# One output unit of a fused attention and feed-forward kernel: three plain output tiles, or two tiles by seven half-size products and a third spread around them

## Chip, cores and metric

The kernel runs on one core of one Trainium2 chip. The metric is the device time of one execution in microseconds. Five runs of the kernel before gave a median of 212.53 us (212.46 to 215.06).

## What is computed

A sparse attention over 4 batches, 8 heads, 768 positions and a head dimension of 64, followed by a feed-forward layer on the 3072 rows of 512 that it gives.

```python
# attention: a window of 16 positions to each side, and 24 block summaries (max of k, mean of v)
k_sum = k.reshape(B, H, nb, 32, D).max(axis=3)
v_sum = v.reshape(B, H, nb, 32, D).mean(axis=3)
scores_l = where(|i - j| < 16, scale * q @ k.T, -1e9)
scores_s = scale * q @ k_sum.T + log(32)
a = softmax(concatenate([scores_l, scores_s]))
x = a @ concatenate([v, v_sum])            # heads side by side: 3072 x 512
# feed-forward
h = x @ w_in                               # 512 -> 2048
out = (h * sigmoid(1.702 * h)) @ w_out     # 2048 -> 512, float32
```

## The kernel before

The 3072 rows are worked in eight units of 384 rows (`HALF`), two to a batch: unit u belongs to batch u // 2, and its half is u % 2. Each unit has three row tiles of 128. `ff_in(u, nts)` multiplies the transposed activations `xT[u % 2]` with `w_in` (64 matmuls of width 384 into the PSUM tiles `ph`) and ScalarE applies the gelu into `gT[u % 2]`.

The second matrix product is done in two ways. `ff_out(u, ms, part)` does a quarter of a plain output tile: four matmuls of width 512 into a PSUM bank `po`; after the fourth quarter ScalarE copies the bank to `osb` and SyncE stores it. `Pair(ta, tb, ss)` forms two row tiles together as a two by two block product by seven half-size products instead of eight (`p1` to `p7`): every product is eight matmuls of width 256, and VectorE forms the sums of the gT quarters (`sums`, into `ss`, and in place in gT), the sums of the `w_out` quarters (`w_sums`, into `ta` and `tb`) and the additions of PSUM results into `osb`. Banks `px`, `pw` and `py` hold running sums. Before the change, units 0 and 1 use `ff_out` throughout, and units 2 to 7 use pairs.

The attention of the next unit or batch is spread between the output steps. After output step `slot` of unit u, `beside(u + 1, slot)` issues what `plan1` (or `plan0`) lists there: `t` transposes q on TensorE, `s` and `S` are `scores` of a pair of heads (12 matmuls listed as `ps_s`, an exponential on ScalarE into `a_sb`, a multiplication with a mask on VectorE), `v` is `values` of two pairs (24 matmuls `ps_av`, then on VectorE a reciprocal and a multiplication for each pair, into `x2`), and `x` transposes the result on TensorE into `xT`. The last results of the stage go to `xT` by transposing transfers, `dx`, issued on SyncE's queue; so do keys (`xk`) and queries (`xq`) of batch 2. POOL's queue loads k, q and v and copies the halo rows of the values inside SBUF (`vw<-vw`, `vw<-vs`).

Order on each engine is the program's order (`_Ordered`). PSUM has eight banks: the pool `pmm`, tag "mm", has four one-bank tiles (`ph`, `po`, `px`, `pw`, `py`, and the small transposes), and the pool `psb`, tag "big", has two two-bank tiles (scores, the q transposes, and value matmuls when `values` is called with `big`). `beside` called `values` with `big` in unit 0's stage (u == 1 there) and without it in unit 1's, the one that is changed:

```python
elif what[0] == "v":
    values(b, half, i, u == 1)
```

Of the kernel before, what the change touches and what calls it, by code (L numbers as in the profile page):

```python
# [11 lines left out]
F16 = mybir.dt.float16  # L12
# [23 lines left out]
def kernel(  # L36
# [25 lines left out]
    JH = NJ // 2  # L62

    pe = _Ordered(tc, nc.tensor)
    dve = _Ordered(tc, nc.vector)
    act = _Ordered(tc, nc.scalar)
# [5 lines left out]
    stage = ctx.enter_context(tc.tile_pool(name="stage", bufs=1))  # L72
# [8 lines left out]
    raw, early = {}, {}  # L81
# [266 lines left out]
    def halo_dmas(w5, j0):  # L348
        halo_odd(w5, j0)
        halo_even(w5, j0)  # L350
# [88 lines left out]
    def q_turn(p, half=0):  # L439
        src = cast.pop(("q", p))  # L440
        ps = pmm.tile([128, 512], F32, name="ps_q", tag="mm")
        st["Q", p] = ps
        for r in range(JH):
            pe.matmul(out=ps[:, r * 128:r * 128 + 128] if half else at(ps, r, [[JH, 128]]),
                      lhsT=src[:, r].rearrange("p h d -> p (h d)"),
                      rhs=ident, start=True, stop=True)
# [136 lines left out]
    def xk(g, b):  # L583
        s = b % 2
        k4 = kxs[s].rearrange("p i (j e) c -> p (i j) e c", e=2)
        src = rows["k", b][:, 2 * g:2 * g + 2].rearrange("p i j h d -> p (i j h d)")
        for e in range(2):
            sp.dma_start(out=k4[:, 2 * g * NJ:2 * (g + 1) * NJ, e, e * 64:e * 64 + 64],
                         in_=src[e * 64:e * 64 + 64], transpose=True)
# [15 lines left out]
    def tq1(p, eng):  # L605
        copy(eng, qT[p][1], trans(rows["q", 1][:, p].rearrange("p j h d -> p j (h d)")))
# [13 lines left out]
    def values(b, half, g, big=False):  # L620

        pvs = []
        for i in range(2):
            p = 2 * g + i
            a = a_sb[p]
            if big and i == 0:
                ps = psb.tile([128, 1024], F32, name="ps_av", tag="big")
            one = (ps[:, i * 512:i * 512 + 512] if big else
                   pmm.tile([128, 512], F32, name="ps_av", tag="mm"))
            pv = one[:, 0:390].rearrange("p (h j c) -> p h j c", h=2, j=JH)  # L630
            pvs.append(pv)
            for hh in range(2):
                for j in range(JH):
                    for e in range(2):
                        t = 2 * j + e
                        pe.matmul(out=pv[e * 64:e * 64 + 64, hh, j, :], lhsT=a[:, hh, t, :],
                                  rhs=vw[b % 2][:, half * TH + t, 2 * p + hh, 0:D + 1],
                                  start=True, stop=True, skip_group_check=True)
        x2[g] = attp.tile([128, 2, JH, 2, D], F16, name="x2", tag="x2")
        for i in range(2):  # L640
            norm(x2[g][:, i], pvs[i])

    def norm(x, pv):
        rc = attp.tile([128, 2, JH, 1], F32, name="rc", tag="rc")
        dve.reciprocal(out=rc, in_=pv[..., D:D + 1])
        dve.tensor_mul(x.rearrange("p j h d -> p h j d"), pv[..., 0:D],
                       rc.to_broadcast([128, 2, JH, D]))
# [42 lines left out]
    def ff_out(u, ms, part):  # L690
        if part == 0:
            po_now[ms] = pmm.tile([128, d_model], F32, name="po", tag="mm")
        po = po_now[ms]
        for nt in range(4 * part, 4 * part + 4):
            pe.matmul(out=po, lhsT=gT[u % 2][:, nt, ms * 128:(ms + 1) * 128],
                      rhs=w_out_sb[:, nt, :], start=(nt == 0), stop=(nt == NT - 1))
        if part == 3:
            osb = outp.tile([128, d_model], F32, name="osb", tag="osb")
            act.activation(out=osb, in_=po, func=ACT.Copy)
            r0 = u * HALF + ms * 128  # L700
            sp.dma_start(out=out[r0:r0 + 128, :], in_=osb)

    NI, DH = NT // 2, d_model // 2
    ts = {}

    def w_sums(c):

        if c == 0:
            w = w_out_sb.rearrange("p (i e) d -> p e i d", e=2)
            b11, b12, b21, b22 = (w[:, e, :, x * DH:(x + 1) * DH] for e in range(2) for x in range(2))  # L710
            ta = stage.tile([128, 2, NI, DH], F16, name="ta", tag="tA")
            tb = stage.tile([128, 2, NI, DH], F16, name="tb", tag="tB")
            ts.update(b11=b11, b12=b12, b21=b21, b22=b22, t1=ta[:, 0], t2=ta[:, 1], t3=tb[:, 0],
                      t4=tb[:, 1])
        for x, y, z in (("t1", "b12", "b11"), ("t2", "b22", "t1"), ("t3", "b22", "b12"),
                        ("t4", "b21", "t2")):
            dve.tensor_sub(*(ts[n][:, 2 * c:2 * c + 2] for n in (x, y, z)))
# [6 lines left out]
    def product(ps, a, b, first):  # L724
        for i in range(NI):
            pe.matmul(out=ps[:, 0:DH], lhsT=a[:, i], rhs=b[:, i], start=(first and i == 0),
                      stop=(i == NI - 1), skip_group_check=True)

    def bank(name):
        return pmm.tile([128, d_model], F32, name=name, tag="mm")  # L730
# [6 lines left out]
    class Pair:  # L737
# [51 lines left out]
            self.w = bank("pw")  # L789
            product(self.w, self.a21, ts["t3"], True)  # L790

        def p2(self):
            y = bank("py")
            product(y, self.a12, ts["b21"], True)
            dve.tensor_add(self.osb(0)[:, 0:DH], y[:, 0:DH], self.t1)
            self.store(0, 0, False)

        def p4(self):
# [8 lines left out]
    def gelu_soon():  # L807

        act.activation(out=gate[:, 1:2], in_=gate[:, 0:1], func=ACT.Gelu_apprx_sigmoid)
# [122 lines left out]
    for p in range(NP):  # L932
# [5 lines left out]


    plan1 = {0: ["t0"], 1: ["t1"], 2: ["s0", "s1"], 4: ["t2"], 5: ["t3"],  # L940
             6: ["v0", "s2", "s3"], 8: ["x0"], 9: ["v1", "S0", "S1"], 11: ["x1", "S2", "S3"]}

    plan0 = {-1: ["q0", "q1", "q2", "q3", "s0", "s1"], 3: ["v0", "s2"], 5: ["x0", "s3"], 7: ["v1"], 9: ["x1"]}

# [2 lines left out]
    def beside(u, slot):  # L947
        b, half = u // 2, u % 2
        for what in (plan0 if u == 1 else plan1).get(slot, ()):
            i = int(what[1])  # L950
            if what[0] == "t":
                tq1(i, dve if i % 2 else act)
            elif what[0] == "q":
                q_turn(i, 1)
                q_copy(i, dve, 1)
            elif what[0] == "s":
                scores(b, half, i)
                if half and i == NP - 1:
                    gelu_soon()
            elif what[0] == "S":  # L960
                scores(b, 1, i)
                if i == NP - 1:
                    gelu_soon()
            elif what[0] == "v":
                values(b, half, i, u == 1)
            else:
                tx(i, half)

    for u in range(2):
        todo = {}  # L970
        if u == 0:
            for p in range(NP):
                todo.setdefault(12 + p // 2, []).append(lambda p=p: cast_q(dve, p, 1))
        else:
            def value_rows():
                vsum(1, range(NJ))
                block_sums()
                halo_dmas(w51, 0)
                sum_dmas(w51, 0)
                load_vc(2)  # L980
                load_qc(2)

            todo = {0: [lambda: tk(0, 1)], 3: [lambda: tk(1, 1)], 5: [lambda: v_odd(1)],
                    6: [lambda: tk(2, 1)], 9: [value_rows], 11: [lambda: tk(3, 1)]}
            ff_in(u, range(3))
        for nt in range(0 if u else N0, NT):
            if u == 0 or nt > 2:
                ff_in(u, (nt,))
            for f in todo.get(nt, ()):
                f()  # L990
        exp_soon()
        if u == 0:
            beside(1, -1)
            load_qc(1)
            load_kc(2)
            busy(6)
        order = [(ms, part) for ms in range(JH) for part in range(4)]
        if u == 0:

            order = [(ms, part) for part in range(4) for ms in range(JH)]  # L1000
        for i, (ms, part) in enumerate(order):
            ff_out(u, ms, part)
            beside(u + 1, i)
            if u == 0 and i in (4, 7, 10):
                w_sums(i // 3 - 1)
            if u == 1 and i == 2:
                w_sums(3)
            if u == 1 and i == 3:
                for g in range(2):
                    xk(g, 2)  # L1010

    order = ["a7", "a2", "a6", "b1", "a5", "b7", "a3", "a4", "b6", "b2", "b5",
             "c1", "b3", "c7", "c6", "c2", "c5", "b4", "c3", "c4"]
# [16 lines left out]
    for b in range(1, B):  # L1030
        n, s = b + 1, (b + 1) % 2
        more = n < B
        ss = stage.tile([128, NP - 1, 2, NI, 128], F16, name="ss", tag="vf")
        u = 2 * b
# [85 lines left out]
```

## Time and profile before

| | |
|---|---|
| Median of five runs | 212.53 us |
| Profiled execution, its own time | 212.8 us |
| Its span, first to last instruction | 210.8 us |
| TensorE clock granted | 1.000 throughout |
| TensorE matmuls busy | 201.6 us, 96% of the span |
| VectorE, ScalarE, POOL busy | 134.3, 122.2, 94.7 us |
| Unit 1's output stage on TensorE | 61.3 to 76.8 us of the span |
| TensorE idle before unit 3 | 1.10 us, waiting for xT |

Times in the text are microseconds from the start of the span unless they are durations. A row of the chain has start, length, engine, tile and number of instructions. A row of a timeline has start, length, engine, operation, tiles out<-in and shape; in brackets stands the idle time before it and what ended it. A matmul row's length includes the drain of the array; the distance between starts is what one costs in a stream.

### The profile page before, as it was taken

To read this page: it belongs to the slowest core of one execution; us is meant where nothing else is said; L and a number is where in the kernel's file an instruction comes from. 1 tells how busy PE (TensorE), PEld (TensorE's weight loads), DVE (VectorE), ACT (ScalarE), POOL (GpSimd) and SP (SyncE) were. 2 spreads that over 40 slices of the span, in tenths; PEclk is the share of its full clock that TensorE was granted. 3 is DMA by queue.
4 is the path that set the end of the run, shared out by engine and by line. 5 is a ranking of instruction groups with operands and counts; after the bars stand their busy time and mean duration, and the time that the engine had idled before them with its cause. 6 is when DMAs were issued, how large, how long until landed. Compare 5 with 4: busy or idle time off the path is not lost.

```text
span 210.8 us, 5499 instructions
## 1 busy us (share of the span) xinstructions
PE 201.6 (96%) x2193; PEld 136.8 (65%) x2193; DVE 134.3 (64%) x394; ACT 122.2 (58%) x228; POOL 94.7 (45%) x173
## 2 busy tenths in 40 slices
PE   7879999999999999899999999999999999999993
PEld 2656565556555556455888875566888865668882
DVE  7489956587976679934767780599757710366332
ACT  2674778155676388657824567677444667772220
POOL 8878989799999931503999201220000000000000
PEclk9999999999999999999999999999999999999999
DMA  5999999999999999999999999992043250000223
GB/s 149 308 164 195 234 252 222 177 149 215 175 160 137 159 151 173 160 162 118 111 126 192 168 180 192 192 132 47 3 137 90 68 159 0 3 0 25 82 77 118
DMA packets 96610, 29.33 MB, mean 139 GB/s; under 512 B 84481, under 2 KB 93601, under 8 KB 96585
## 3 DMA queue, kind: packets, MB, share of 16 engines
q0 software_dynamic: 67920, 14.88, 79.8%
q1 hardware_dynamic: 28664, 14.11, 34.4%
q8 instruction: 17, 0.28, 0.6%
q14 instruction: 9, 0.07, 0.1%
HBM read 27.26 MB, written 6.29 MB: 159 GB/s over the span
## 4 chain that ended last, share of the span: by engine, by line
PE 68%; POOL 13%; DMA 12%; SPq 2%; DVE 2%; issue 2%; POOLq 0%
PE ph L28 28%; PE px L28 15%; PE pw L28 8%; PE po L28 5%; DMA xT<-x 4%; PE py L28 4%; DMA kb<-in_k_dram 3%; PE ps_s L28 3%; PE ps_av L28 3%; POOL qb L28 3%; DMA qf<-in_q_dram 2%; POOL mk L28 2%; POOL kb L28 2%; DMA kq<-in_k_dram 2%; SPq L28 2%
## 5 line engine op out<-in xcount | busy, mean ns | idle before, releaser
L28 PE MATMUL ph<-xT,w_in_sb 128*128 128x384 f16 x512 | 86.3, 326 | 1.2 <-DMA xT<-x 1.1
L28 ACT ACTIVATE gT<-ph 128x384 f16<-128x384 f32 x128 | 61.0, 491 | 27.2 <-PE ph L28 27.0
L28 PEld LDWEIGHTS <-w_in_sb 128*128 128x128 f16 x512 | 49.3, 98 | 33.8 <-DMA xT<-x 1.5
L28 PEld LDWEIGHTS <-gT 128*128 128x128 f16 x384 | 35.6, 98 | 12.4
L28 ACT ACTIVATE a_sb<-ps_s 128x768 bf16<-128x768 f32 x28 | 21.2, 806 | 11.4 <-PE ps_s L28 11.4
L28 PE MATMUL po<-w_out_sb,gT 128*128 128x512 f16 x96 | 23.1, 380 | 0.0
L28 PEld LDWEIGHTS <-ss 128*128 128x128 f16 x216 | 20.9, 98 | 2.6
L28 DVE TENSOR_TENSOR a_sb<-a_sb,mk 128x768 bf16<-128x768 bf16 x28 | 15.6, 557 | 10.0 <-ACT a_sb L28 8.4
L28 DVE TENSOR_TENSOR ss<-gT 128x512 f16<-128x512 f16 (+3 forms) x21 | 8.0, 381 | 21.0 <-ACT gT L28 20.9
L28 ACT ACTIVATE t<-px 128x256 f32<-128x256 f32 x21 | 8.1, 385 | 20.2 <-PE px L28 20.2
L28 PE MATMUL pw<-tb,gT 128*128 128x256 f16 x144 | 18.7, 273 | 0.0
L28 PE MATMUL px<-ta,ss 128*128 128x256 f16 x144 | 18.7, 273 | 0.0
L28 DVE TENSOR_REDUCE ks<-kx 128x24 bf16<-128x768 bf16 x12 | 11.3, 945 | 8.1 <-DMA kx<-kb 8.1
L28 POOL DMA_DIRECT2D vw<-vw x12 | 6.5, 558 | 22.2 <-DVE vw L28 14.3
L28 DVE TENSOR_TENSOR x<-ps_av,rc 128x384 f16<-128x384 f32 x28 | 15.6, 558 | 1.0
L28 POOL DMA_DIRECT2D vw<-in_v_dram x18 | 15.9, 933 | 0.0
L28 POOL DMA_DIRECT2D kb<-in_k_dram x16 | 13.2, 851 | 1.9 <-DMA w_out_sb<-in_moe_w_out_dram 1.4
L28 POOL DMA_DIRECT2D qb<-in_q_dram x16 | 13.3, 928 | 1.1 <-DMA vw<-in_v_dram 1.1
L28 DVE TENSOR_TENSOR osb<-pw,t 128x256 f32<-128x256 f32 x18 | 7.6, 423 | 9.2 <-PE pw L28 5.1
L28 ACT ACT_TABLE_LOAD x10 | 12.8, 1283 | 1.0 <-PEq L1104 0.8
L28 PE MATMUL ps_s<-qT,kx 64*128 64x64 bf16 (+3 forms) x400 | 9.5, 190 | 1.0 <-DVE qT L28 1.0
L28 PEld LDWEIGHTS <-kx 64*128 64x128 bf16 x400 | 7.4, 94 | 4.6 <-issue 3.9
(103 smaller groups left out, 247.0 us busy)
## 6 DMA issues: line engine op xcount, KB each, us to landing
out_dram<-osb SPq DMA_DIRECT2D x18, 256.0 KB, 5.0
vw<-in_v_dram POOLq DMA_DIRECT2D x18, 128.0 KB, 5.4
w_in_sb<-in_moe_w_in_dram POOLq DMA_DIRECT2D x4, 512.0 KB, 8.9
w_out_sb<-in_moe_w_out_dram POOLq DMA_DIRECT2D x4, 512.0 KB, 16.8
kf<-in_k_dram SPq DMA_DIRECT2D x8, 192.0 KB, 4.3
kb<-in_k_dram POOLq DMA_DIRECT2D x16, 96.0 KB, 4.7
qb<-in_q_dram POOLq DMA_DIRECT2D x16, 96.0 KB, 7.1
out_dram<-osb SPq DMA_DIRECT2D x12, 128.0 KB, 1.7
```

Source lines behind the costliest of these rows:

```text
L28: r = f(*a, **kw)
```

## The change

In unit 1, row tiles 0 and 1 are formed by a `Pair`, and tile 2 by `ff_out`, with its four quarters as steps 2, 3, 4 and 11 of the twelve. `sums` of the pair and its first addition (`c11`, split off from `p2`) follow step 1. The last part of the weight sums, `w_sums(3)`, moves ahead of the stage. One step holds no output work. In `plan1`, `x0` moves from step 8 to 7, and `v1`, `S0`, `S1` from 9 to 8. `values` always takes a "big" PSUM tile. The key transposes `xk` of batch 2 stay after step 3, but no output tile is finished by then. The sums take the staging buffer "vf" before batch 1's pairs use it.

```diff
-        def p2(self):
-            y = bank("py")
-            product(y, self.a12, ts["b21"], True)
-            dve.tensor_add(self.osb(0)[:, 0:DH], y[:, 0:DH], self.t1)
+        def p2(self, early=False):
+            self.y = bank("py")
+            product(self.y, self.a12, ts["b21"], True)
+            if not early:
+                self.c11()
+
+        def c11(self):
+            dve.tensor_add(self.osb(0)[:, 0:DH], self.y[:, 0:DH], self.t1)
             self.store(0, 0, False)
...
     plan1 = {0: ["t0"], 1: ["t1"], 2: ["s0", "s1"], 4: ["t2"], 5: ["t3"],
-             6: ["v0", "s2", "s3"], 8: ["x0"], 9: ["v1", "S0", "S1"], 11: ["x1", "S2", "S3"]}
+             6: ["v0", "s2", "s3"], 7: ["x0"], 8: ["v1", "S0", "S1"], 11: ["x1", "S2", "S3"]}
...
             elif what[0] == "v":
-                values(b, half, i, u == 1)
+                values(b, half, i, True)
...
-        order = [(ms, part) for ms in range(JH) for part in range(4)]
         if u == 0:
-
-            order = [(ms, part) for part in range(4) for ms in range(JH)]
-        for i, (ms, part) in enumerate(order):
-            ff_out(u, ms, part)
-            beside(u + 1, i)
-            if u == 0 and i in (4, 7, 10):
-                w_sums(i // 3 - 1)
-            if u == 1 and i == 2:
-                w_sums(3)
-            if u == 1 and i == 3:
-                for g in range(2):
-                    xk(g, 2)
+            for i in range(12):
+                ff_out(0, i % JH, i // JH)
+                beside(1, i)
+                if i in (4, 7, 10):
+                    w_sums(i // 3 - 1)
+
+    ss = stage.tile([128, 2, NI, 128], F16, name="ss", tag="vf")
+    pair = Pair((1, 0), (1, 1), ss)
+    w_sums(3)
+    for i, step in enumerate(("p2", "p1", 0, 1, 2, "p7", "p6", "p5", None, "p3", "p4", 3)):
+        if step == "p2":
+            pair.p2(True)
+        elif step == "p1":
+            pair.p1(act)
+        elif step in (0, 1, 2, 3):
+            ff_out(1, 2, step)
+        elif step:
+            getattr(pair, step)()
+        beside(2, i)
+        if i == 1:
+            pair.sums(0, NI)
+            pair.c11()
+        if i == 3:
+            for g in range(2):
+                xk(g, 2)
```

## Prediction

> **What bounds the kernel now.** I read the busy shares first, then the chain that ended last, then the waits of the stage that is edited, then ScalarE, SyncE and the transfers beside it. All instructions go through one helper (L28), so groups are told apart by tile.
>
> ```profile
> span 210.8 us, 5499 instructions
> PE 201.6 (96%) x2193; PEld 136.8 (65%) x2193; DVE 134.3 (64%) x394; ACT 122.2 (58%) x228; POOL 94.7 (45%) x173
> ```
>
> TensorE is the bound: whatever shortens or stalls its list moves the end. The chain, in order of time (start, length, what), shows the edited stage (output of unit 1, 61.3 to 76.8) and what follows:
>
> ```profile
> 62.48 0.86 PE po L28 x4
> ...
> 69.23 0.50 PE ps_av L28 x24
> 69.73 0.46 PE ps_s L28 x24
> 70.19 1.83 PE po L28 x8
> 72.02 0.34 PE ps_x L28 x6
> ...
> 79.74 2.60 PE ph L28 x16
> 82.33 8.81 DMA xT<-x
> 91.19 9.59 PE ph L28 x58
> 100.77 0.87 PE px L28 x8
> ```
>
> Inside the stage TensorE goes from one piece to the next without a gap. The chain leaves it only at 82.33: unit 3 waits for its transposed activations xT. TensorE's timeline shows the price, and the list of transfers their time to landing:
>
> ```profile
> 89.95 2.37 PE L28 MATMUL ph<-xT,w_in_sb 128*128 128x384 f16 x12 [1.10 <-DMA xT<-x]
> ```
>
> ```profile
> xT<-x SPq DMA_TRANSPOSE x2, 8.9
> ```
>
> 1.10 us before 89.95, and, since the second tile landed 0.25 us after the first six matmuls, 1.35 us in all. So a shift of TensorE before 88.85 isn't simply a shift of the end: 1.35 us here belong to the transfers. Beside TensorE in the stage, ScalarE and SyncE's queue:
>
> ```profile
> 64.87 1.51 ACT L28 ACTIVATE a_sb<-ps_s 128x768 bf16<-128x768 f32 x2 [0.84 <-PE ps_s L28]
> ...
> 70.06 1.51 ACT L28 ACTIVATE a_sb<-ps_s 128x768 bf16<-128x768 f32 x2 [2.04 <-PE ps_s L28]
> ```
>
> ```profile
> 66.90 0.33 SPq L28 DMA_DIRECT2D out_dram<-osb  x1
> 67.47 8.67 SPq L28 DMA_TRANSPOSE kx<-kq  x4
> 76.23 2.16 SPq L28 DMA_DIRECT2D out_dram<-osb  x2
> 80.95 2.86 SPq L28 DMA_TRANSPOSE xT<-x  x2
> ```
>
> Two score groups are exponentiated one behind the other (0.81 us each, 0.70 apart) while TensorE has 1.8 us of output matmuls to do. SyncE's queue is in order: the four key transposes stand behind the first output store, which waited for ScalarE's copy of the first tile.
>
> **The change, part by part.**
>
> *TensorE's products.* Removed: 12 chunks of four 512-wide matmuls at 0.86 to 0.87 (chain rows), 10.4. Added: seven products of eight 256-wide matmuls at 0.87 (row px x8), 6.1, and four chunks, 3.45. Gain 0.85 us; bounds 0.8 and 0.9. Each 256-wide matmul needs its own weight load, 98 ns by the page's group of ss loads, under the 109 ns that a matmul lasts, so nothing is added. The Trainium skill, TensorE: Matmul & The Clock Gate, section Back-to-back issue gap, speaks against the change: it gives sustained spacings of 81 ns at width 128 and 131 ns at 512, hence, as an estimate between, some 97 ns at 256; by it 56 x 97 + 16 x 131 stand against 48 x 131 and the change would lose 1.2 us. This trace has 216 ns at 512 and 109 at 256, and decides.
>
> *First product.* py needs odd gT columns up to the last gelu, which ends at 61.81; its eighth matmul would come at 61.9. Up to 0.15 us; I take 0.1.
>
> *VectorE and ScalarE.* Added on VectorE: three sums of 128x1024 and one more in p6 (0.67 to 0.69 each on the three rows at 89.59), three adds of 0.42 from PSUM, 4.0 us; w_sums(3) only moves forward, to 61.8. VectorE is busy 11.4 of 17.7 us here, so 15.4 fit. The last sum (a21, which p7 reads) ends near 66.3 and p7 starts near 67.1: covered by 0.8 us, and each 0.1 beyond costs 0.1. ScalarE gets four copies of 0.385 for two of 0.60: +0.3, in idle time.
>
> *Score buffers: the new wait.* The value matmuls now take a "big" PSUM tile, of which there are two, instead of two "mm" banks (those hold px, pw, po and the transposes). In plan1, v0, s2, s3 follow each other without TensorE work between, and so do v1, S0, S1. The value tile is held until VectorE has normalised it (1.5 us, rows at 69.58 to 71.06), so both score groups share the other buffer: in the built program's order the first matmul of the second group waits for ScalarE, the exponential of the first. From 64.48, the first score matmul, to 64.87 is 0.39, the exponential 0.81, a semaphore 0.04: the second group can start 1.24 after the first where it now starts at 0.23. That is 1.0 us, twice: 2.0. Behind it on TensorE's in-order list stands the rest of the stage. Bounds: 0 if the buffers were given out otherwise, 2 x 1.5 if a group waited for the normalisation instead; the order names ScalarE, so 2.0.
>
> *Late masks.* s3 is late, so its exponential and mask (0.81 + 0.56) end 1.8 after its matmuls begin; p5, x0 and the first half of v1 cover 0.23 + 0.87 + 0.34 + 0.25 = 1.7. Wait 0.1 to 0.4; I take 0.3. S0, S1 have p3, p4 and a chunk behind them: nothing; without these it would be 1.8 too.
>
> *SyncE's queue and the halos.* POOL's list is unchanged, its key, halo and value transfers from 53 to 70 included; SyncE keeps the same number, but no output store stands ahead of the key transposes. They wait only for k of batch 2, whose first four heads land by 61.5. So they issue from 61.8 rather than 67.5 and meet the value halos that v0 needs (vw<-vw, vw<-vs, the last landing 67.55 against v0 at 69.2: cover 1.6). The trace doesn't show this meeting. Nearest rows: two halo copies issued at 126.15 near transposes landed in 5.4 us against 4.9 (+0.5: no wait); those at 86.3 to 89.3, behind a backlog, took 8.2 to 10.6 against 4 to 5 (+3.4 to +6.4: a wait of 1.8 to 4.8). It is nearer the first in backlog, the second in number of transposes: +2.4, wait 0.8. Cover gone, each us late is a us. The Trainium skill, DMA: Bandwidth & Descriptors, section Queues, rings and completion order, says that an engine alternates between queues packet by packet, a half share. By that, an estimate: 4.2 us of halo traffic left would take 8.4 and v0 wait 2.6.
>
> *The xT wait.* Unit 2 now starts 0.85 less and 0.1 + 2.0 + 0.3 + 0.8 more, 2.35 us later; its transposes issue at 83.3 and 84.7, and TensorE reaches unit 3 at 91.2. No wait if the first lands within 7.9 us and the second within 7.5. Bounds: 2.8 us (the transpose at 155.28, little beside it) and 8.9 as now. Now the key transposes hold the queue until about 82 and two stores until 86; begun 5.7 us earlier, they end near 75 and three stores follow by about 82. I take under 7.5: the 1.35 goes. If not, it stays. Stores, q loads and xT share the same engines, but what is moved is the same in sum.
>
> Sum: -0.85 + 0.1 + 2.0 + 0.3 + 0.8 - 1.35 = +1.0 us. The profiled execution took 212.8, 2.0 around its span; it is 0.27 above the median of 212.53, so I add the sum to the median: 213.5.
>
> **Rivals.** (a) xT still takes 8.9 us, as the queue is only reshuffled: no slack comes back, +2.35, 214.9. For it: DMA engines are busy in nine tenths or more of nearly all of 61 to 92; against: the queue ahead is shorter. (b) Halos come 3 us after v0's turn, as behind the backlog at 86: +3.2, 215.7, and up to 217.5 at 4.8. (c) No halo wait, the rest as forecast: +0.2, 212.7; for it the row at 126.15. (d) Faster: the two score groups get separate buffers, so the one exchange of banks costs nothing. Then the stage is 0.85 - 0.1 shorter and the xT wait also falls: -0.75 - 1.35 = -2.1, 210.4. It decides as soon as the second score matmul starts within 0.3 us of the first; the program's order speaks against it. (e) That the products don't save their columns: the widths are in the list; no share.
>
> **How the numbers follow.** Forecast 0.42, with a range of its own from 212.8 to 214.7; (a) 0.26; (b) 0.15; (c) 0.11; (d) 0.06. A measurement of this kernel can tell about 1% from no change, 2.1 us: 210.4 to 214.65. Faster: half of (d), 0.03. Slower: (a), (b) and 0.04 of the forecast's upper edge, 0.45. Same: 0.52. The range leaves out (d), the upper third of (b) and a little of (c): 212.5 to 216.3.
>
> **What would show it.** In the profile after: two TensorE gaps near 1.0 us ahead of score matmuls, released by ScalarE's a_sb; a gap of 0.3 ahead of value matmuls, and one ahead of v0 released by a vw transfer; key transposes from about 61.8; unit 2's first ph near 79.1 instead of 76.73; no gap at unit 3. Wrong if the score groups stand side by side, if the xT gap is still over 1 us, or if v0 doesn't wait.

## The result, and the profile after

Against the kernel before, the changed kernel took 1.0084 of the time (95% interval 1.0062 to 1.0106), which on the median of 212.53 us is 214.3 us; measured again beside two variants it was 1.0071 (1.0038 to 1.0105). That is 0.8% more: the interval lies above 1, but the step is under the 1% within which the forecast called a kernel the same. (The comparison uses only executions within 1.5% of the fastest of each kernel; the plain medians over all of them, 216.69 us after and 213.19 before, lie 1.6% apart, because it leaves out 23 of 40 executions after and 7 of 77 before.)

The profiled execution took 214.23 us. Its page, the span and the busy shares:

```profile
span 212.5 us, 5559 instructions
PE 201.7 (95%) x2217; PEld 140.0 (66%) x2217; DVE 136.5 (64%) x401; ACT 122.7 (58%) x230; POOL 94.2 (44%) x173
```

TensorE is busy 201.7 us where it was 201.6, although work was saved, and the span is 1.7 longer. The first reason is not in the edited stage. A table by stretches (stretch, its length, busy time of PE, PEld, DVE, ACT and POOL, the granted clock, the DMA share, GB/s) has half clock long before it, in code that both kernels share:

```profile
12.00:16.40 4.40, 3.25 (x72) 2.31 (x71) 3.89 (x8) 3.35 (x4) 3.58 (x10) 1.00 2.15 170
16.40:19.90 3.50, 3.23 (x60) 1.99 (x60) 1.96 (x4) 0.81 (x1) 3.43 (x6) 0.51 1.23 200
```

Unit 1's output stage therefore starts at 62.31 instead of 61.12, 1.19 us late. So I count places in the stage from its first matmul, here the first `py`, before the first `po`. TensorE's timeline of the stage:

```profile
62.31 1.04 PE L28 MATMUL py<-w_out_sb,gT 128*128 128x256 f16 x8
...
70.39 0.57 PE L28 MATMUL ps_av<-vw,a_sb 128*64 128x65 bf16 x24
70.89 0.35 PE L28 MATMUL ps_s<-qT,kx 64*128 64x64 bf16 x12
72.14 0.35 PE L28 MATMUL ps_s<-qT,kx 64*128 64x64 bf16 x12 [0.90 <-ACT a_sb L28]
...
75.55 0.35 PE L28 MATMUL ps_s<-qT,kx 64*128 64x64 bf16 x12 [0.90 <-ACT a_sb L28]
...
79.34 2.12 PE L28 MATMUL ph<-xT,w_in_sb 128*128 128x384 f16 x12
```

The 24 score matmuls that stood together before are now two groups of 12 with 0.90 us of idle time between them, twice, both ended by ScalarE's exponential. Unit 2's first `ph` comes 17.03 us after the stage's first matmul; before it came after 15.61. The stage has grown by 1.42. The chain that ended last now goes through those two waits, and then stays on TensorE where it used to leave for xT:

```profile
71.28 0.82 ACT a_sb L28
72.10 0.04 issue
72.14 0.35 PE ps_s L28 x12
...
74.69 0.82 ACT a_sb L28
...
87.45 12.62 PE ph L28 x77
```

SyncE's queue shows what was moved: the key transposes first, the stores behind them in one block, then xT. The second row is from the list of transfers (tile, queue, count, median time from issue to landing):

```profile
61.78 9.27 SPq L28 DMA_TRANSPOSE kx<-kq  x4
77.39 2.22 SPq L28 DMA_DIRECT2D out_dram<-osb  x3
83.55 2.60 SPq L28 DMA_TRANSPOSE xT<-x  x2
```

```profile
xT<-x SPq DMA_TRANSPOSE x2, 5.0
```

xT lands 5.0 us after its issue instead of 8.9, and unit 3 no longer waits: the 1.35 us of before are gone. At the first output product after units 2 and 3, `px`, the profile is 39.38 us from the stage's start, and the kernel before was 39.49: 0.11 us faster, not slower. Its longer span is nearly all the 1.19 us ahead of the stage and a wait of 0.51 us for xT at unit 4. So this one profile doesn't show where 0.8% went. It has an expected wait missing, that of the value matmuls for their halos: the half clock held TensorE back by 1.2 us at the stage's start, and the last halo landed at 70.15, just ahead of the matmuls at 70.39. The experiments look there.

### The profile page after: what moved, and what is told of

Read it like the earlier page. It is cut to its first block, busy times and chain, and to the rows that moved or that the text cites. A ratio compares the mean times of both kernels' runs of the same rounds, so it can differ in the third digit from the quotient of the medians.

```text
span 212.5 us, 5559 instructions
## 1 busy us (share of the span) xinstructions
PE 201.7 (95%) x2217; PEld 140.0 (66%) x2217; DVE 136.5 (64%) x401; ACT 122.7 (58%) x230; POOL 94.2 (44%) x173
## 3 DMA queue, kind: packets, MB, share of 16 engines
q0 software_dynamic: 67920, 14.88, 81.6%
## 4 chain that ended last, share of the span: by engine, by line
PE 66%; DMA 20%; POOL 6%; SPq 2%; DVE 2%; issue 1%; ACT 1%; POOLq 0%
PE ph L28 30%; PE px L28 16%; DMA w_out_sb<-in_moe_w_out_dram 9%; PE pw L28 7%; DMA xT<-x 4%; PE py L28 4%; DMA kb<-in_k_dram 3%; POOL qb L28 3%; PE ps_s L28 3%; PE ps_av L28 2%; DMA qf<-in_q_dram 2%; SPq L28 2%; DMA kq<-in_k_dram 2%; PE po L28 2%; PE ps_t L28 1%
## 5 line engine op out<-in xcount | busy, mean ns | idle before, releaser
L28 PEld LDWEIGHTS <-ss 128*128 128x128 f16 x240 | 23.1, 98 | 2.8
L28 ACT ACTIVATE t<-px 128x256 f32<-128x256 f32 x24 | 9.2, 385 | 21.7 <-PE px L28 21.7
L28 DVE TENSOR_TENSOR ss<-gT 128x512 f16<-128x512 f16 (+3 forms) x22 | 8.7, 394 | 19.4 <-ACT gT L28 19.4
L28 PE MATMUL pw<-tb,gT 128*128 128x256 f16 x160 | 20.9, 273 | 0.0
L28 PE MATMUL px<-ta,ss 128*128 128x256 f16 x160 | 20.8, 273 | 0.0
L28 PE MATMUL po<-w_out_sb,gT 128*128 128x512 f16 x64 | 15.2, 380 | 0.0
L28 DVE TENSOR_TENSOR osb<-pw,t 128x256 f32<-128x256 f32 x20 | 8.5, 423 | 9.7 <-PE pw L28 5.5
L28 PE MATMUL ps_s<-qT,kx 64*128 64x64 bf16 (+3 forms) x400 | 10.0, 192 | 2.8 <-ACT a_sb L28 1.8
```

What stands on the lines that cost most here:

```text
L28: r = f(*a, **kw)
```

## Experiments

**One buffer exchange alone.** The kernel before, with nothing changed but the PSUM tile of the values:

```diff
-                values(b, half, i, u == 1)
+                values(b, half, i, True)
```

> The kernel before, with one edit: the value matmuls of unit 1's stage take a big PSUM tile, as after the change; no pair, no moved step. Theory (the shared score buffer costs the stage its time): two TensorE gaps of 0.9 to 1.0 us ahead of the second score group of each pair of groups, released by ScalarE's a_sb, unit 2's first ph 2.0 us later than 76.7, and, since the key transposes still stand behind the first output store, the wait for xT before unit 3 stays at 1.0 to 1.4 us: time +1.9 us, +0.9%. Rival (the stage's growth comes from the products and their VectorE work): no gap there, time within 0.2% of before.

Ratio 1.0038 (1.0000 to 1.0076). TensorE's timeline:

```profile
71.98 0.35 PE L28 MATMUL ps_s<-qT,kx 64*128 64x64 bf16 x12 [0.90 <-ACT a_sb L28]
...
77.05 0.35 PE L28 MATMUL ps_s<-qT,kx 64*128 64x64 bf16 x12 [0.90 <-ACT a_sb L28]
```

One argument brings both score waits into the old kernel. Unit 2 starts 17.77 after the stage's first matmul, 2.16 later than before; that is the price of the exchange. But the time grew by less, 0.8 us, because unit 3's wait of 1.35 was gone, and I had expected it to stay. In this kernel the key transposes are as late as before, so their place in the queue is not what removes the wait for xT. 2.16 less 1.35 is 0.81, and the ratio's 0.4% is 0.8 us.

**The early keys alone.** The kernel before, with the key transposes issued one step earlier, ahead of the first output store:

```diff
             if u == 1 and i == 2:
                 w_sums(3)
-            if u == 1 and i == 3:
                 for g in range(2):
                     xk(g, 2)
```

> The kernel before, with one edit: the four key transposes of batch 2 are issued one step earlier, so that no output store stands ahead of them on SyncE's queue. Theory (the order of that queue alone makes the xT wait): key transposes from about 61.8 instead of 67.5, xT lands in 5 to 7.5 us instead of 8.9, the 1.35 us ahead of unit 3 are gone, no wait for the halos: time -1.3 us, -0.6%. Rival (the transfers are limited by their sum, the order changes nothing): xT still takes 8.5 us or more and the time stays within 0.2%. Second rival: the halos are late and the value matmuls wait 0.8 us: -0.5 us.

Ratio 1.0003 (0.9970 to 1.0036); the 1.3 us less that I expected did not come. The value matmuls now wait for the halo copies; the row of transfers below it is for those issued from 62 to 65 us, and the last fence has the same row of the kernel before:

```profile
70.27 0.79 PE L28 MATMUL ps_av<-vw,a_sb 128*64 128x65 bf16 x24 [1.40 <-DMA vw<-vs]
```

```profile
vw<-vs POOLq DMA_DIRECT2D x2, 148.5 KB, 7.3
```

```profile
vw<-vs POOLq DMA_DIRECT2D x2, 148.5 KB, 4.0
```

Beside the transposes the same copies take 7.3 us instead of 4.0. TensorE loses 1.40 waiting, and 0.22 more in the value matmuls behind the wait (0.79 instead of 0.57). Unit 2 starts 17.30 after the stage's first matmul, 1.69 later, and nearly all of it comes back at unit 3, which doesn't wait. A loss of 1.7 us in the stage and no change in the time that the interval can show: without the trace this run would have said that the early keys cost nothing.

**The whole change, keys held back.** The changed kernel with a transfer of two columns on SyncE's queue that reads the second pair's masked scores (`a_sb[1]`), so that the key transposes behind it issue from 68.4:

```diff
+    held_k = consts.tile([128, 2], BF16, name="held_k")
...
         if i == 3:
+            sp.dma_start(out=held_k, in_=a_sb[1][:, 0, 0, 0:2])
             for g in range(2):
                 xk(g, 2)
```

> The kernel after, with one edit: a transfer of 2 values of pair 1's masked scores into a spare tile stands ahead of the key transposes on SyncE's queue and waits for VectorE's mask, so that they issue at about 68 as before the change. Theory: xT takes 8.5 to 9 us again, the wait ahead of unit 3 is back with 1.0 to 1.4 us, the rest as after: +1.3 us over after, +1.4% over before. Rival (xT landed in time because of something else in the change, such as the two stores that come later): no wait ahead of unit 3, time as after.

Ratio 0.9992 (0.9959 to 1.0024): the 0.8% are gone. TensorE's waits from 60 to 100 us (engine and tile, who ended the wait, total, times, longest) are one line:

```profile
PE ps_s L28 <- ACT a_sb L28: 1.8, 2, 0.9
```

The score waits stand, the halos land at 68.66 or before, and unit 2 starts at +17.03. Against my expectation unit 3 again doesn't wait for xT. So the changed kernel's loss of 0.8% is, within the intervals, that of the early key transposes, and the two score waits, 2.16 us, are paid by the saved products and by the slack that xT had.

**The changed kernel once more,** for a profile whose early part has full clock.

> The changed kernel once more, for a profile whose early part runs at full clock and for a time beside the others of this set. Halo theory: the key transposes issue near 61.5, the last value halo lands near 70.3 and the first value matmuls, whose turn comes 8.08 us after the stage's first matmul (69.2), wait 1.1 to 1.4 us. With two score waits of 0.90, unit 2 starts 18.2 us after the stage's first matmul (15.61 in the kernel before); unit 3 does not wait for xT. Sum against before: +2.6 - 1.35 = +1.2 us, ratio 1.006. Rival: the early transposes cost nothing in the stage and the kernel is only slowed by stretches at half clock that lie elsewhere; then no wait ahead of the value matmuls, unit 2 at +17.0, and a ratio of 1.000.

Ratio 1.0071, as expected of the halo theory. The profiled execution took 217.06 us; it shows the place of the wait, not its mean size. Its timeline, and the table by stretches behind the wait:

```profile
72.28 0.83 PE L28 MATMUL ps_av<-vw,a_sb 128*64 128x65 bf16 x24 [2.76 <-DMA vw<-vs]
```

```profile
73.00:77.00 4.00, 3.10 (x46) 2.37 (x38) 2.44 (x6) 1.97 (x3) 2.72 (x4) 0.61 2.55 142
```

The wait for the halos is there, 2.76 us in this execution, and a stretch at half clock follows it (0.50 from about 73.9 to 77.3; the row's 0.61 is the mean over a wider stretch). Both together put unit 2 at +21.39, where 18.2 was expected.

**The early keys where nothing can be given back.** The changed kernel, with the q loads of batch 2 on POOL's queue held until the x that goes into unit 3's xT is formed (a copy of two columns that reads it stands ahead of them), so that they are out of xT's way:

```diff
-                load_qc(2)
...
+            def queries_later():
+                pool.tensor_copy(out=after, in_=x2[1][:, 0, 0, 0, 0:2])
+                load_qc(2)
...
-                     4: [lambda: dx(1, 1)]}
+                     4: [lambda: dx(1, 1), queries_later]}
```

> The changed kernel with the q loads of batch 2 held until after the transposing transfers of xT, and the key transposes early as in the change. Beside the earlier run with held q loads and late keys (ratio 0.9989) it prices the early key transposes with xT's slack out of the way. Halo theory: the value matmuls wait 1.1 to 1.4 us for the last halo, xT lands 4 to 5 us after issue and unit 3 does not wait, so nothing is given back: 1.0 to 1.4 us over the earlier run, ratio to before 1.004 to 1.006. Rival (the early transposes cost nothing): 0.999.

Ratio 1.0044 (1.0014 to 1.0074). With the keys late as well, a kernel of the next group measured 0.9989 (0.9952 to 1.0026). The early keys cost 0.55%, 1.2 us, within what was expected, though the two intervals together leave 0.15 to 2.2 us. xT lands 4.0 us after its issue and unit 3 doesn't wait. The profiled execution, 219.49 us, had two waits for halos, 1.98 and 3.30; so this wait has no fixed size.

**What xT waits for.** First the kernel before with only the q loads held, the same edit:

> The kernel before, with one edit: POOL's eight loads of q for batch 2 are held until the last value rows of unit 1 are normalised (about 82 instead of 70 to 79). Theory (xT lands when the backlog of transfers is drained, near 90, whenever it was issued; the runs so far have it at 89.1 to 91.1 for issues from 82.3 to 86.3): without the q loads in the backlog xT lands about 4 us after its issue, near 85 and 86, before TensorE reaches unit 3 at 88.85; the wait of 1.35 us goes: -1.3 us, -0.6%. Rival (xT needs 8.9 us by itself): no change.

Ratio 0.9948 (0.9910 to 0.9987), 1.1 us, near the 1.35. xT was issued at 81.14, as before, and the list of transfers has

```profile
xT<-x SPq DMA_TRANSPOSE x2, 3.9
```

for 8.9. Unit 3 doesn't wait; unit 4 has a new wait of 0.37 for its own xT, and 1.35 less 0.37 is 1.0. Then the other side, a stage that is shorter, with the q loads left where they were: the spread order (told below) with the keys held back.

> The steps of the spread version with the key transposes held behind the first masked scores, q loads as in the kernel before. The stage itself is then 0.3 us shorter than in the kernel before (no score wait, no halo wait, 0.85 us of products saved less small shifts): unit 2 starts 15.3 us after the stage's first matmul. Backlog theory: xT still lands at 89.5 to 90.5, because the transfers queued ahead of it are drained only then, so unit 3 waits 1.3 to 1.8 us and the time is that of the kernel before: ratio 0.999, within 0.002. Rival (the shift of the key transposes in the queue is what took xT's wait away, or it takes a fixed time from its issue): no wait at unit 3, 0.3 + 1.35 us less, ratio 0.992.

Ratio 1.0055 (1.0016 to 1.0094), worse than the backlog theory said and far from the rival's 0.992. The stage is short as expected (unit 2 at +15.29), xT is issued at 80.04, and TensorE's timeline and table have

```profile
88.36 1.15 PE L28 MATMUL ph<-xT,w_in_sb 128*128 128x384 f16 x6 [0.41 <-DMA xT<-x]
91.81 10.98 PE L28 MATMUL ph<-xT,w_in_sb 128*128 128x384 f16 x58 [2.29 <-DMA xT<-x]
```

```profile
91.80:95.20 3.40, 3.39 (x13) 1.65 (x13) 0.00 (x0) 1.65 (x4) 0.00 (x0) 0.58 1.29 156
```

xT is no earlier for being issued earlier. It waits 2.7 us in all, and the 58 matmuls behind the wait take 10.98 us instead of 9.59, since a stretch at half clock follows (0.50 from about 91.3 to 94.7). Set side by side, the mean issue time of the two tiles plus the time to landing:

| kernel | mean issue | to landing | lands at | unit 3 waits |
|---|---|---|---|---|
| spread, keys late | 81.1 | 8.9 | 90.0 | 2.70 |
| before | 81.6 | 8.9 | 90.5 | 1.35 |
| before, keys early | 83.0 | 7.0 | 90.0 | 0 |
| after, keys late | 83.4 | 6.1 | 89.5 | 0 |
| after | 84.2 | 5.0 | 89.2 | 0 |
| before, shared buffer | 84.9 | 4.8 | 89.7 | 0 |
| before, q loads held | 81.8 | 3.9 | 85.7 | 0 |

In the first six the issue moves by 3.8 us and the landing by 1.3. In the seventh the transfers ahead of it are gone, and from the same issue time as in the kernel before it lands 4.8 us sooner. Two more profiles with the q loads in their place issue xT later still: the spread order with early keys at 85.6 (landing at 88.7) and the changed kernel again at 87.7 (92.1, 4.4 after the issue); unit 3 waits in neither. For issues up to 85 xT is a wall at about 90 us, set by the q loads queued ahead of it, and a stage that ends up to 1.35 us later reaches unit 3 without a loss.

**With the wall moved: the changed kernel, keys late and q loads held.**

> The kernel after with both cures: key transposes held until pair 1's masks (about 68), and the q loads held until about 84. Theory: no wait for halos, none for xT, so that the stage's own growth is bare: +1.5 us over h_before (15.6 to 17.0 us from its first matmul to unit 2's first), two waits of 0.9 us ahead of score matmuls; +0.2 us over before, +0.1%. Rival (the growth of the stage is made up elsewhere, or costs nothing): time as h_before.

Ratio 0.9989 (0.9952 to 1.0026), as expected: the two score waits cost what the products and xT's slack give. Against the kernel before with the same held q loads (0.9948) it is 0.4% slower, 0.9 us, but the two intervals overlap. The profiles show the loss of the change by itself, without the halos' part and without xT's slack: 1.42 us of stage, less the 0.37 at unit 4 that only the other kernel waits, 1.05.

**One of the two pairs of score groups apart.** The same kernel, the sixth score pair a step later, with `p3` between it and the fifth:

```diff
-             6: ["v0", "s2", "s3"], 7: ["x0"], 8: ["v1", "S0", "S1"], 11: ["x1", "S2", "S3"]}
+             6: ["v0", "s2", "s3"], 7: ["x0"], 8: ["v1", "S0"], 9: ["S1"], 11: ["x1", "S2", "S3"]}
```

> h_after with one edit: the scores S1 come one step later, behind p3. Theory: the wait ahead of them shrinks from 0.9 to 0.1 us and nothing takes its place, as their mask isn't read before unit 2: 0.85 us less than h_after; -0.3% against before. Rival (TensorE waits for ScalarE's list wherever S1 stands): as h_after.

Ratio 0.9956 (0.9918 to 0.9994). The second gap is gone and unit 2 starts at +16.17 instead of +17.03; this the profile shows, while the interval still overlaps that of the kernel it is compared with. The profile has lost part of it again, at a place that none of the edits touches, unit 4:

```profile
125.53 9.58 PE L28 MATMUL ph<-xT,w_in_sb 128*128 128x384 f16 x58 [2.05 <-DMA xT<-x]
```

**No shared score buffer in either pair.** The third and fourth groups now stand a step apart, and the fifth and sixth have a buffer each. First with the change's early keys and unheld q loads:

```diff
-    for i, step in enumerate(("p2", "p1", 0, 1, 2, "p7", "p6", "p5", None, "p3", "p4", 3)):
+    for i, step in enumerate(("p2", "p1", 0, 1, 2, "p7", "p6", "p5", "p3", "p4", 3, None)):
...
-             6: ["v0", "s2", "s3"], 7: ["x0"], 8: ["v1", "S0", "S1"], 11: ["x1", "S2", "S3"]}
+             6: ["v0", "s2"], 7: ["s3"], 8: ["x0"], 9: ["v1", "S0", "S1"], 11: ["x1", "S2", "S3"]}
...
-                values(b, half, i, True)
+                values(b, half, i, not (u == 2 and i in (1,)))
```

> The kernel after with its steps in another order: p2, p1, 0, 1, 2, p7, p6, p5, p3, p4, 3, and the empty step last; s3 comes a step after s2, x0 after p3, v1, S0, S1 after p4, and v1 takes two mm banks, free by then, so S0 and S1 have a buffer each. Theory (the two 0.9 us score waits are what the change loses): both gaps go, some 0.2 us each remain at s3, p3 and x1, unit 2's first ph at 76.5 instead of 78.2 in after's own terms, xT in time: 1.4 us under before, -0.6%, and 2.0 under after. Rival (half-size products or VectorE's additions cost the stage as much): time as after.

Ratio 1.0035 (0.9998 to 1.0073), where 0.994 was expected. The score waits went, and the value matmuls, whose turn comes no later than before, waited for the halos in two pieces:

```profile
70.51 0.19 PE L28 MATMUL ps_av<-vw,a_sb 128*64 128x65 bf16 x1 [1.87 <-DMA vw<-vs]
72.19 0.54 PE L28 MATMUL ps_av<-vw,a_sb 128*64 128x65 bf16 x23 [1.49 <-DMA vw<-vs]
```

Then the same order with late keys and held q loads:

> The steps of e9_spread (s3 a step after s2, x0 after p3, v1 with two mm banks, S0 and S1 in a buffer each, chunk 3 ahead of the empty step), with the key transposes held until about 68 and the q loads until about 82. Theory: no score wait, no wait for halos, none for xT; the stage takes 15.4 to 15.6 us, as before the change, as 0.85 us of saved columns meet some 0.7 us of short waits (s3, p3, x1, first product): -1.3 to -1.5 us against before, -0.65%, level with h_before or 0.1 us under it. Rival (something else in the pair costs TensorE 1 us or more): as h_after.

Ratio 0.9951 (0.9905 to 0.9998). This version and the one with `S1` apart (0.9956) are the only ones with the new products whose intervals lie below the kernel before, if barely. TensorE's waits from 55 to 140 us come to one, 0.19 us:

```profile
71.08 1.03 PE L28 MATMUL px<-w_out_sb,ss 128*128 128x256 f16 x8 [0.19 <-ACT t L28]
```

Unit 2 starts at +15.30, 0.31 sooner than in the kernel before. In time it can't be told from the kernel before with held q loads (0.9948): of the 0.88 us that the products save, the stage keeps 0.31 even in this form.

## Why the prediction was right, and where it was not

The predicted 213.5 us lay 0.8 under the 214.3 that the ratio gives, inside the forecast's own range (212.8 to 214.7). Its terms:

- *Products, -0.85.* Measured -0.88: from one start to the next on the timelines, twelve plain quarters take 10.68 us before, seven products and four quarters 9.80 after. The trace's 216 and 109 ns held.
- *First product, +0.1.* Nothing: `py` takes 0.87 from its start to the next piece, as `po` did.
- *Score buffers, +2.0.* 2.16. The idle time is 0.90 twice, as worked out from the exponential; from its start to the next piece a double score group takes 1.53 where it took 0.45. The first kernel of the experiments shows the same 2.16 alone. Rival (d), separate buffers, is out.
- *VectorE and ScalarE, nothing.* The last sum ends at 67.40 and `p7` starts at 68.21, the 0.8 us of cover that was forecast.
- *Late masks, +0.3.* 0.16 at most: the second value matmuls stretch by 0.07 without a gap, and one set of transposes by 0.09 (0.42 for 0.33). No run shows that the masks cause the second part; the kernel before has 0.43 for the set at 75.85.
- *Halos, +0.8.* This is the term that was mis-sized. In the kernel before with early keys it is 1.69: 1.40 of wait, 0.22 in slower matmuls behind it, 0.07 elsewhere. In the changed kernel the ratio's 1.79 us leave 1.7 for it (1.79 + 0.88 - 2.16 - 0.16 + 1.35), 1.2 to 2.2 by the interval, together with any half clock that follows the wait. I had set the meeting of copies and transposes between two rows of the trace, and nearer the mild one; the copies took 7.3 us where that guess gave 6.4. Rival (b), 3 us late, named the right place, and too much for the ratio. Single executions range widely: the profiles with early keys have 0, 1.40, 2.76, 3.36 (1.87 + 1.49) and 5.28 us (1.98 + 3.30). The Trainium skill, DMA: Bandwidth & Descriptors, section Queues, rings and completion order, states the turns packet by packet; my estimate of 2.6 from them, by a half share of the time, lies within this range and above the 1.7 of the ratio. The row of the trace that I trusted more was too low. Rival (c), no halo wait, is what the first profile after shows, with TensorE 1.2 us late at the stage; the rerun has the wait.
- *xT, -1.35.* Right in size, wrong in its reason. I put it down to the key transposes leaving SyncE's queue earlier. But in the kernel before the queue's rows end at 78.39, and xT is issued at 80.95, after 2.5 us of waiting for VectorE's x: the queue did not hold it back. And in two kernels where they stay late, the wait goes as well. What removes it is that the stage ends later while xT lands at the same 90 us. Rival (a), 8.9 us from any issue, fails for the same cause.

With measured sizes the sum is -0.88 + 0 + 2.16 + 0.16 + 1.69 - 1.35 = +1.8 us, which is the ratio. The wrong reason for xT's wait cost nothing here, and that was luck. It would have cost the forecast of a change that shortens this stage: by it the time would fall, and by the runs it meets the wall.

Of the signs, three came: two gaps near 1.0 (0.90 each), key transposes from 61.78, no gap at unit 3. The gap of 0.3 ahead of value matmuls did not. The gap at the first value matmuls, whose absence I had named as a sign of being wrong, was absent from the first profile and present in the second. Unit 2 at 79.34 is near the forecast's 79.1 only by luck: the stage began 1.19 us late and had no halo wait, so that it grew by 1.42 us where 2.35 was forecast.

A cost that no term had is at unit 4: 0.51 us of waiting for its xT in the profile after, none before. It is 0.37, 0.46, 0.69 and 2.05 in kernels that have little in common there and absent in others; what sets it was not tried.

## What to carry to other kernels

When a transfer is awaited at a time that doesn't follow its issue, find the time at which the work ahead of it is drained: until then a delay upstream is free, and a gain upstream is worth nothing. Before moving a transfer in a queue that waits for an earlier one, look at what it will run beside; the loss here came from four key transposes that no matmul of this stage was waiting for. And a ratio of 1.000 can hold 1.7 us lost in one stage and 1.35 found in the next, so read the waits of each stage as well as the time.

## What was not expected of the hardware

A wait can cost more than its length. Behind TensorE waits of 0.41 + 2.29 us (the spread order with late keys), 2.76 us (the changed kernel again) and 1.87 + 1.49 us (the spread order with early keys) the granted clock was 0.50 for about 3.4 us, and behind 1.98 + 3.30 us (early keys, q loads held) for about 6.8 us; in the first, 58 matmuls took 1.39 us longer for it. Behind 1.40 and 2.05 us it stayed at 1.00. The Trainium skill, TensorE: Matmul & The Clock Gate, section Part 1: The HAM clock gate, has half rate follow an idle window of about 3.4 us that runs freely; the length of the slow stretch agrees, while here half rate also came behind waits that were each shorter than such a window. That it was the wait that set off the stretch was not tested by itself; in the profile after there is one at 16.4 with no wait over 0.9 us just ahead of it.

The halo copies' time beside DMA transposes was not only longer but uneven: 3.8 to 4.7 us in the eight profiles with the transposes later, 6.5, 7.3, 7.7, 7.9 and 8.8 in the five with them early.
